# Half-height score matmuls for two heads into two PSUM banks side by side, in an attention kernel followed by two linear layers

One NeuronCore of one Trainium2 chip runs the whole program. The metric is the device time of one execution in microseconds (us); lower is better. The profile's span leaves out about 2 us of it. In the profile PE is TensorE (matmuls), ACT is ScalarE, DVE is VectorE and POOL is GpSimd. Matmuls write their results to a memory called PSUM, of which the pools below take eight banks; a pool hands out tiles, that is, named pieces of memory.

## The reference, cut to what matters

```python
def _attn_ref(q, k, v):                      # 8 batches, 8 heads, 576 positions, 64 per head
    scores = scale * np.matmul(q, k.transpose(0, 1, 3, 2))
    # heads 0 to 3: a band of 32 positions; heads 4 to 7: every 32nd position, causal
    scores = np.where(masks[None], scores, -1e9)
    ...                                      # softmax along the last axis
    return np.matmul(attn, v)

def _moe_ref(x, w_in, w_out, alpha):         # x: 4608 x 512, hidden 2048
    h = x @ w_in
    g = np.maximum(h, 0.0) + alpha * np.minimum(h, 0.0)
    return g @ w_out
```

The attention output, 4608 rows of 512, is the input of the two layers.

## The kernel before

Attention works on pairs of heads: a batch has two "local" pairs (6 blocks of 96 queries) and two "strided" ones (8 blocks of 72). Queries lie in `qpad`, where each head has its 64 rows and zeros in the other 64, so one matmul over 128 rows gives the scores of both heads:

```python
pspool = ...tile_pool(name="ps", bufs=5, space=PSUM)   # one bank each: tp, tt, sp, pv, xp
phpool = ...tile_pool(name="ph", bufs=2, space=PSUM)   # one bank each: first layer
popool = ...tile_pool(name="po", bufs=1, space=PSUM)   # second layer
# score_piece: 2 or 3 blocks, up to 432 columns, one bank
sp = pspool.tile([128, 512], F32, tag="ps", name="sp")
for x, t in enumerate(grp):
    matmul(sp[:, 2*w*x : 2*w*x + 2*w], P.kT[:, k0 : k0+128], P.qpad[:, :, w*t : w*t + w], ...)
...
activation(et[0:r, 0:n], sp[0:r, 0:n], AF.Exp, scale=SCALE)
# lin1_piece: 4 matmuls of 512 columns, then ReLU on ScalarE, then a fused op on VectorE
hps = phpool.tile([128, 512], F32, tag="hps", name="hps")
...
activation(neg, hps, AF.Relu, scale=-1.0)
scalar_tensor_tensor(gTs[n][:, m, :], neg, oma[:, m:m+1], hps, op0=mult, op1=add)   # a step later
```

In the dense part of the program a piece of the second layer, a step of attention, a piece of the first layer and another step of attention follow each other. A step of attention transposes q or k, makes scores, transposes an output, or multiplies weights by v (PV). Waits between engines are put in by the framework, from the tiles that each instruction reads and writes.

The softmax here doesn't subtract the row's maximum and nothing guards it: scores larger than these inputs give would overflow.

## Time and profile before

| | before |
|---|---|
| time | 373.56 us, median of 3 (372.94 to 374.19) |
| TensorE busy | 337.2 of 371.5 us (91%) |
| VectorE, ScalarE, POOL busy | 61%, 53%, 38% |
| chunk 0, chunk 1 of the first layer start | 36.99, 72.65 us |

A linear piece is one sixteenth of a chunk of 512 rows. The first is a line of the waits view: who waited for whom, us in total, times, longest. The second is TensorE's timeline (start, us, engine, line, what) near the end, where no attention is left.

```profile
PE hps L493 <- DVE gT L506: 0.7, 4, 0.2
```

```profile
295.41 1.03 PE L538 MATMUL ops<-wout,gT 128*128 128x512 f16 x4
296.27 1.03 PE L493 MATMUL hps<-xT,win 128*128 128x512 f16 x4
297.14 1.03 PE L538 MATMUL ops<-wout,gT 128*128 128x512 f16 x4
```

The first layer's two accumulators are enough: TensorE hardly ever waits for VectorE to empty one. One piece of each layer takes 297.14 - 295.41 = 1.73 us, with nothing between.

### The profile page before, as it was taken

The page shows a single profiled execution, that of the slowest core. Times are in us where ns is not written, and L with a number is a line of the kernel's source. Part 1 is how long each engine was busy: PE and PEld are TensorE (multiplying, and loading weights), DVE is VectorE, ACT ScalarE, POOL GpSimd, SP SyncE. Part 2 cuts the span into 40 slices and gives each one's busy share as a digit, 9 for nine tenths or more (in the row PEclk, how much of TensorE's full clock was granted, in tenths as well). Part 3 has the DMA queues.
Part 4 walks back from the last instruction along what each step waited for, and adds up shares of the span by engine and source line. Part 5 has one row for each costly group of instructions (what it writes and reads, how often), then busy time and mean ns, then how long its engine had stood idle before and what let it go on. Part 6 is the DMA issues. An engine that isn't in the chain of part 4 may idle for free.

```text
span 371.5 us, 6466 instructions
## 1 busy us (share of the span) xinstructions
PE 337.2 (91%) x2505; PEld 187.8 (51%) x2505; DVE 226.2 (61%) x442; ACT 195.4 (53%) x364; POOL 142.4 (38%) x189
## 2 busy tenths in 40 slices
PE   7677984897694999999999999999999999999996
PEld 2354443544452555555557767555555444444444
DVE  4265787488566567767776768685866544444410
ACT  2425675467345357564756585658565443353421
POOL 7274435204989364654655443335233000000000
PEclk9979998899999699999999999999999999999999
DMA  8999999915497377337535503100000001001012
GB/s 164 75 163 201 172 197 159 100 9 64 76 123 119 48 90 100 63 75 78 94 60 95 64 28 80 38 30 31 28 30 28 30 28 58 29 34 53 28 56 86
DMA packets 46779, 28.66 MB, mean 77 GB/s; under 512 B 27276, under 2 KB 41980, under 8 KB 46748
## 3 DMA queue, kind: packets, MB, share of 16 engines
q0 software_dynamic: 40944, 18.06, 43.6%
q1 hardware_dynamic: 5804, 10.19, 7.7%
q8 instruction: 19, 0.31, 0.4%
q14 instruction: 12, 0.10, 0.1%
HBM read 36.86 MB, written 9.44 MB: 125 GB/s over the span
## 4 chain that ended last, share of the span: by engine, by line
PE 72%; DMA 10%; ACT 6%; DVE 5%; POOL 4%; issue 2%; POOLq 0%; ACTq 0%
PE ops L538 30%; PE hps L493 29%; PE sp L287 4%; DMA k<-in_k_dram 3%; DMA wout<-in_moe_w_out_dram 3%; ACT kT L142 3%; PE pv L329 3%; PE tp L195 3%; DMA vl<-in_v_dram 2%; PE xp L346 2%; DMA q<-in_q_dram 2%; DVE x L338 2%; ACT neg L503 1%; PE ops L529 1%; DVE vl L144 1%
## 5 line engine op out<-in xcount | busy, mean ns | idle before, releaser
L493 PE MATMUL hps<-xT,win 128*128 128x512 f16 (+1 forms) x640 | 144.8, 359 | 1.0 <-DVE gT L506 0.7
L538 PE MATMUL ops<-wout,gT 128*128 128x512 f16 x560 | 142.9, 381 | 0.4 <-ACT osb L543 0.4
L506 DVE SCALAR_TENSOR_TENSOR gT<-neg,oma,hps 128x512 f16<-128x512 f32 x144 | 107.0, 743 | 53.5 <-ACT neg L503 50.0
L503 ACT ACTIVATE neg<-hps 128x512 f32<-128x512 f32 x144 | 86.0, 597 | 89.5 <-PE hps L493 87.7
L315 POOL TENSOR_TENSOR et<-et,consts 128x384 f16<-128x384 f16 (+2 forms) x60 | 54.3, 913 | 82.5 <-ACT et L307 81.7
L493 PEld LDWEIGHTS <-win 128*128 128x128 f16 x640 | 59.7, 98 | 50.0 <-issue 2.6
L538 PEld LDWEIGHTS <-gT 128*128 128x128 f16 x560 | 50.3, 98 | 46.1 <-issue 1.0
L307 ACT ACTIVATE et<-sp 128x384 f16<-128x384 f32 (+2 forms) x96 | 45.2, 489 | 23.7 <-PE sp L287 17.5
L287 PE MATMUL sp<-qpad,kT 128*128 128x144 f16 (+1 forms) x224 | 32.4, 241 | 13.9 <-DVE kT L144 4.5
L338 DVE TENSOR_TENSOR x<-pv,rc 72x384 f16<-72x384 f32 (+2 forms) x80 | 42.2, 527 | 2.7
L144 DVE COPY qpad<-tp 64x512 f16<-64x512 f16 (+1 forms) x44 | 37.7, 857 | 3.9 <-PE tp L195 1.9
L336 DVE RECIPROCAL rc<-pv 72x6 f32<-72x6 f32 (+2 forms) x80 | 14.8, 186 | 39.7 <-PE pv L329 39.5
L287 PEld LDWEIGHTS <-kT 128*128 128x128 f16 x224 | 20.0, 100 | 34.7 <-issue 7.3
L142 ACT COPY kT<-tp 64x512 f16<-64x512 f16 (+2 forms) x36 | 27.5, 765 | 14.8 <-PE tp L195 12.4
L329 PEld LDWEIGHTS <-et 72*128 72x128 f16 (+1 forms) x448 | 24.5, 100 | 20.9 <-issue 5.7
L543 ACT COPY osb<-ops 128x512 f32<-128x512 f32 x35 | 20.5, 586 | 20.1 <-PE ops L538 20.1
L560 PE MATMUL wps<-wrm 128*128 128x512 f16 x48 | 19.7, 479 | 1.2 <-DVE wrm L573 1.2
L102 POOL DMA_DIRECT2D q<-in_q_dram x16 | 11.9, 745 | 20.3 <-PE tp L195 15.1
L329 PE MATMUL pv<-vl,et 128*128 128x65 f16 x192 | 12.1, 195 | 6.3 <-DVE vl L144 3.8
L346 PE MATMUL xp<-consts,x 72*128 72x72 f16 (+1 forms) x224 | 15.5, 209 | 1.8 <-DVE x L338 1.7
L346 PEld LDWEIGHTS <-x 72*128 72x128 f16 (+1 forms) x224 | 12.9, 104 | 8.2 <-DVE x L338 3.1
L329 PE MATMUL pv<-vs,et 72*128 72x65 f16 x256 | 16.1, 199 | 0.1
(61 smaller groups left out, 205.9 us busy)
## 6 DMA issues: line engine op xcount, KB each, us to landing
out_dram<-osb SPq DMA_DIRECT2D x35, 256.0 KB, 2.0
q<-in_q_dram POOLq DMA_DIRECT2D x16, 256.0 KB, 5.3
k<-in_k_dram POOLq DMA_DIRECT2D x16, 256.0 KB, 5.9
vl<-in_v_dram POOLq DMA_DIRECT2D x8, 288.0 KB, 6.2
win<-in_moe_w_in_dram POOLq DMA_DIRECT2D x4, 512.0 KB, 8.2
wout<-in_moe_w_out_dram POOLq DMA_DIRECT2D x4, 512.0 KB, 13.0
stv<-in_v_dram POOLq DMA_DIRECT2D x7, 288.0 KB, 5.4
stv<-in_v_dram SPq DMA_DIRECT2D x1, 576.0 KB
```

The source lines that it names most:

```text
L142: keep(nc.scalar.copy(o, i))
L144: keep(nc.vector.tensor_copy(o, i))
L287: keep(nc.tensor.matmul(sp[:, 2 * w * x : 2 * w * x + 2 * w], P.kT[:, k0 : k0 + 128], P.qpad[:, :, w * t : w * t + w], start=(x == 0), sto ...
L307: keep(nc.scalar.activation(et[0:r, 0:n], sp[0:r, 0:n], AF.Exp, scale=SCALE))
L315: keep(nc.gpsimd.tensor_tensor(ev, ev, m.unsqueeze(1).to_broadcast([r, n // w, w]), op=ALU.mult))
L329: keep(nc.tensor.matmul(pv[:, 65 * x : 65 * x + 65], et[0:r, c : c + 128], v16[0:r, 2 * P.pr + hh, t, :] if P.strided else v16[:, 6 * (2 * ...
L338: keep(nc.vector.tensor_tensor(P.x16[0:w, c0 : c0 + 64 * nb].rearrange("r (c e) -> r c e", e=64), pvv[:, :, 0:64], rc[0:w, 0:nb].unsqueeze ...
L346: keep(nc.tensor.transpose(xp[:, P.w * t : P.w * t + P.w], P.x16[0 : P.w, 128 * t : 128 * t + 128], ident[0 : P.w, 0 : P.w]))
L493: keep(nc.tensor.matmul(hps[:, dst : dst + w], win16[:, kk, 128 * m : 128 * m + 128], xT[:, kk, src : src + w], start=(kk == 0 and x == 0) ...
L503: keep(nc.scalar.activation(neg, hps, AF.Relu, scale=-1.0))
L506: keep(nc.vector.scalar_tensor_tensor(gTs[n][:, m, :], neg, oma[:, m : m + 1], hps, op0=ALU.mult, op1=ALU.add))
L538: keep(nc.tensor.matmul(ops, gTs[n][:, kf, 128 * mt : 128 * mt + 128], wout16[:, kf, :], start=(kf == 0), stop=(kf == 15)))
```

## The change

It wants fewer and larger instructions around the scores. Heads of a pair sit in rows 0 to 63 and 64 to 127 of a compact `qT`, and each gets its own matmul of half height into its own bank; one exponential and one mask multiplication then cover both banks, 576 columns of each pair at a time, twice per pair instead of three times. Copies into a padded q go. Local q and k come in as fp32 and are cast on POOL; memsets, loads and the order of attention pieces change too. Because a score block takes two banks, the eight banks are dealt out anew.

```diff
-    pspool = ... tile_pool(name="ps", bufs=5, PSUM)
-    phpool = ... tile_pool(name="ph", bufs=2, PSUM)
+    pspool = ... tile_pool(name="ps", bufs=3, PSUM)
+    phpool = ... tile_pool(name="ph", bufs=1, PSUM)
+    pbpool = ... tile_pool(name="pb", bufs=1, PSUM)
+    sb = pbpool.tile([128, 2, 512], F32, name="sb")
+    hb = phpool.tile([128, 2, 512], F32, name="hb")
 ... (score_piece)
-        sp = pspool.tile([128, 512], F32, tag="ps", name="sp")
+        sp = hb if wide["on"] and ectr["i"] % 2 else sb
-            matmul(sp[:, 2*w*x : 2*w*x + 2*w], P.kT[:, k0 : k0+128], P.qpad[:, :, w*t : w*t+w], ...)
+            for y in range(2):
+                hf = slice(64*y, 64*y + 64)
+                matmul(sp[:, y, w*x : w*x + w], P.kT[hf, k0 : k0+128], P.qT[hf, w*t : w*t+w], ...)
-        activation(et[0:r, 0:n], sp[0:r, 0:n], AF.Exp, scale=SCALE)
+        activation(ev.rearrange("r (y c) -> r y c", y=2), sp[0:r, :, 0:n], AF.Exp, scale=SCALE)
 ... (lin1_piece)
-            hps = phpool.tile([128, 512], F32, tag="hps", name="hps")
+            hps = hb[:, m % 3 if alone else m % 2]
 ... (copies, loads, casts, memsets, order of pieces: cut)
```

`wide` is on while attention runs with no linear layer beside it.

More of the change, by code (lines that the diff above doesn't have):

```diff
@@ L27, in _build_consts @@
     ident = np.eye(128, dtype=np.float16)
-    return np.concatenate([ident, first, first, other, other, mstr], axis=1)
+    return np.concatenate([ident, first, other, other, mstr], axis=1)
 @with_exitstack
@@ L62 @@
     opool = ctx.enter_context(tc.tile_pool(name="op", bufs=3))
-    pspool = ctx.enter_context(tc.tile_pool(name="ps", bufs=5, space=bass.MemoryType.PSUM))
-    phpool = ctx.enter_context(tc.tile_pool(name="ph", bufs=2, space=bass.MemoryType.PSUM))
+    pspool = ctx.enter_context(tc.tile_pool(name="ps", bufs=3, space=bass.MemoryType.PSUM))
+    phpool = ctx.enter_context(tc.tile_pool(name="ph", bufs=1, space=bass.MemoryType.PSUM))
+    pbpool = ctx.enter_context(tc.tile_pool(name="pb", bufs=1, space=bass.MemoryType.PSUM))
     popool = ctx.enter_context(tc.tile_pool(name="po", bufs=1, space=bass.MemoryType.PSUM))
@@ L72 @@
     ))
-    consts = cpool.tile([128, 584], F16)
+    consts = cpool.tile([128, 488], F16)
     id16 = cpool.tile([16, 16], F32)
@@ L76 @@
     oma = cpool.tile([128, 16], F32)
-    madd = cpool.tile([128, 456], F16)
+    madd = cpool.tile([128, 360], F16)
     ident = consts[:, 0:128]
-    mfirst, mother, mstr = consts[:, 128:512], consts[:, 320:416], consts[0:72, 512:584]
+    mfirst, mother, mstr = consts[:, 128:416], consts[:, 224:320], consts[0:72, 416:488]
     win16 = cpool.tile([128, 4, 2048], F16)
@@ L83 @@
     xT = cpool.tile([128, 4, RING], F16)
-    NE = 8
-    qpads = [cpool.tile([128, 2, 2, S], F16, name=f"qpad{i}") for i in range(2)]
+    NE = 6
+    qTs = [cpool.tile([128, 2, S], F16, name=f"qT{i}") for i in range(2)]
     kTs = [cpool.tile([128, 2, 672], F16, name=f"kT{i}") for i in range(2)]
@@ L89, with load_qk, cast_l @@
     vss = [cpool.tile([128, 4, 8, 65], F16, name=f"vs{i}") for i in range(2)]
-    ets = [cpool.tile([128, 512], F16, name=f"et{i}") for i in range(NE)]
+    ets = [cpool.tile([128, 640], F16, name=f"et{i}") for i in range(NE)]
     loaded = {}
     cast16 = {}
-    def load_qk(b, strided):
+    def load_qk(b, strided, nm):
         h0 = 4 if strided else 0
-        for nm, src in (("q", q), ("k", k)):
-            t16 = hpool.tile([128, 2, 512], F16, tag=f"{nm}16", name=f"{nm}16")
-            base = src[b, h0 : h0 + 1, 0:1, :]
-            keep(nc.gpsimd.dma_start(t16, bass.AP(
-                tensor=base.tensor, offset=base.offset,
-                ap=[[8 * D, 64], [2 * S * D, 2], [S * D, 2], [1, 8 * D]])))
-            cast16[(b, strided, nm)] = t16
+        src = q if nm == "q" else k
+        if strided:
+            t16 = hpool.tile([128, 2, 512], F16, tag=f"{nm}s", bufs=3, name=f"{nm}s")
+            cast16[(b, True, nm)] = t16
+        else:
+            t16 = hpool.tile([128, 2, 512], F32, tag=f"{nm}l", bufs=2, name=f"{nm}l")
+            loaded[(b, nm)] = t16
+        base = src[b, h0 : h0 + 1, 0:1, :]
+        eng = nc.sync if b > 2 and not strided else nc.gpsimd
+        keep(eng.dma_start(t16, bass.AP(
+            tensor=base.tensor, offset=base.offset,
+            ap=[[8 * D, 64], [2 * S * D, 2], [S * D, 2], [1, 8 * D]])))
+    def cast_l(b, nm, eng="pool"):
+        t16 = hpool.tile([128, 8, 2, 64], F16, tag=f"{nm}l16", bufs=2, name=f"{nm}l16")
+        cast_copy(eng, t16, loaded[(b, nm)].rearrange("p f (t d) -> p t f d", t=8))
+        cast16[(b, False, nm)] = t16
     def load_tail(b, strided):
@@ L165 @@
     ectr = {"i": 0}
-    q_rest = []
+    wide = {"on": True}
+    sb = pbpool.tile([128, 2, 512], F32, name="sb")
+    hb = phpool.tile([128, 2, 512], F32, name="hb")
     NEARLY = 2
@@ L175, in make_pair @@
         u = g // 2
-        P.qpad, P.kT = qpads[u % 2][:, g % 2], kTs[u % 2][:, g % 2]
-        P.sgroups = ([0, 1, 2], [3, 4, 5], [6, 7]) if P.strided else ([0, 1], [2, 3], [4, 5])
-        P.pgroups = P.sgroups if P.strided else ([0, 1, 2], [3, 4, 5])
+        P.qT, P.kT = qTs[u % 2][:, g % 2], kTs[u % 2][:, g % 2]
+        P.sgroups = ([0, 1, 2, 3], [4, 5, 6, 7]) if P.strided else ([0, 1, 2], [3, 4, 5])
+        P.pgroups = ([0, 1, 2], [3, 4, 5], [6, 7]) if P.strided else P.sgroups
         P.et = {}
@@ L190, in transpose_piece @@
         src = cast16[(b, strided, nm)]
-        qpad, kT = qpads[u % 2], kTs[u % 2][:, :, 32:608]
+        dst = qTs[u % 2] if nm == "q" else kTs[u % 2][:, :, 32:608]
         tp = pspool.tile([128, 8, 64, 2], F16, tag="ps", name="tp")
         for j in range(8):
-            t, f = j // 2, j % 2
-            keep(nc.tensor.transpose(
-                tp[:, j].rearrange("r p e -> r (p e)"), src[:, f, 128 * t : 128 * t + 128], ident))
-        half = [slice(0, 64), slice(64, 128)]
+            blk = (src[:, j % 2, 128 * (j // 2) : 128 * (j // 2) + 128] if strided
+                   else src[:, j].rearrange("p f d -> p (f d)"))
+            keep(nc.tensor.transpose(tp[:, j].rearrange("r p e -> r (p e)"), blk, ident))
@@ L199, in transpose_piece @@
         if strided:
             main = tp.rearrange("r j p e -> r e j p")
-            def q_copy(par, es, eng):
-                o = qpad[half[par], es, par, :].rearrange("r e (j p) -> r e j p", j=8)
-                cast_copy(eng, o[:, :, :, 0:64], main[half[par], es])
-            def k_copy(es, eng):
-                o = kT[:, es].rearrange("r e (j p) -> r e j p", j=8)
-                cast_copy(eng, o[:, :, :, 0:64], main[:, es])
-        else:
-            main = tp.rearrange("r (t f) p e -> r f e p t", f=2)
-            def q_copy(f, par, eng):
-                o = qpad[half[f], :, f, 0:512].rearrange("r e (p t c) -> r e p t c", t=4, c=2)
-                cast_copy(eng, o[:, :, :, :, par], main[half[par], f])
-            def k_copy(f, par, eng):
-                o = kT[half[f], :, 0:512].rearrange("r e (p t c) -> r e p t c", t=4, c=2)
-                cast_copy(eng, o[:, :, :, :, par], main[half[par], f])
@@ L222, in transpose_piece @@
-        e0, e1, both = slice(0, 1), slice(1, 2), slice(0, 2)
-        if nm == "q":
-            if strided and early:
-                q_copy(0, e0, "dve")
-                q_copy(1, e0, "act")
-                q_rest.append(lambda: (q_copy(0, e1, "dve"), q_copy(1, e1, "act")))
-            elif strided:
-                q_copy(0, both, "dve")
-                q_copy(1, both, "dve")
-            else:
-                for f in range(2):
-                    for par in range(2):
-                        q_copy(f, par, "act" if early and par else "dve")
+            o = dst.rearrange("r e (j p) -> r e j p", j=8)[:, :, :, 0:64]
+        else:
+            main = tp.rearrange("r t p e -> r e p t")
+            o = dst[:, :, 0:512].rearrange("r e (p t) -> r e p t", t=8)
@@ L235, in transpose_piece, with tails @@
+        if early:
+            for e in range(2):
+                eng = "dve" if (nm == "q") == (e == 0) else "act"
+                if nm == "k" and e == 1:
+                    tails(b, u, strided)
+                cast_copy(eng, o[:, e : e + 1], main[:, e : e + 1])
             return
+        cast_copy("dve" if nm == "q" else "act", o, main)
+        if nm == "k":
+            tails(b, u, strided)
+    def tails(b, u, strided):
         tl = cast16[(b, strided, "tail")]
@@ L246, in transpose_piece @@
                     tt[:, 128 * e : 128 * e + 128], tl[:, 128 * e : 128 * e + 128], ident))
-        def tails():
+        for i, (o, eng) in enumerate(((qTs[u % 2], "dve"), (kTs[u % 2][:, :, 32:608], "act"))):
             if strided:
                 tv = tt[:, 0:256].rearrange("r (e f i p t) -> r i e t f p", e=2, f=2, i=2, p=8)
-                ov = lambda o: o.rearrange("r e (t f p) -> r e t f p", t=4, f=2)
+                ov = o.rearrange("r e (t f p) -> r e t f p", t=4, f=2)
                 for e in range(2):
-                    keep(nc.scalar.copy(ov(kT)[:, e, :, :, 64:72], tv[:, 1, e]))
-                for par in range(2):
-                    for e in range(2):
-                        keep(nc.vector.tensor_copy(
-                            ov(qpad[half[par], :, par, :])[:, e, :, :, 64:72],
-                            tv[half[par], 0, e]))
+                    cast_copy(eng, ov[:, e, :, :, 64:72], tv[:, i, e])
@@ L259, in tails @@
             else:
                 tv = tt[:, 0:256].rearrange("r (e i p) -> r i e p", e=2, i=2)
-                keep(nc.scalar.copy(kT[:, :, 512:576], tv[:, 1]))
-                for f in range(2):
-                    keep(nc.vector.tensor_copy(qpad[half[f], :, f, 512:576], tv[half[f], 0]))
-        if strided and early:
-            k_copy(e0, "act")
-            tails()
-            q_rest.pop()()
-            k_copy(e1, "dve")
-        elif strided:
-            k_copy(both, "act")
-            tails()
-        else:
-            for f in range(2):
-                for par in range(2):
-                    k_copy(f, par, "dve" if early and par else "act")
-            tails()
+                cast_copy(eng, o[:, :, 512:576], tv[:, i])
@@ L279, in score_piece @@
     def score_piece(P, i):
         et = ets[ectr["i"] % NE]
+        sp = hb if wide["on"] and ectr["i"] % 2 else sb
         ectr["i"] += 1
-        sp = pspool.tile([128, 512], F32, tag="ps", name="sp")
-        w = P.w
-        grp = P.sgroups[i]
+        w, grp = P.w, P.sgroups[i]
+        n = w * len(grp)
+        r = 72 if P.strided else 128
+        early = P.b < NEARLY
         for x, t in enumerate(grp):
             k0 = 32 + 72 * t if P.strided else 96 * t
-            keep(nc.tensor.matmul(
-                sp[:, 2 * w * x : 2 * w * x + 2 * w], P.kT[:, k0 : k0 + 128],
-                P.qpad[:, :, w * t : w * t + w], start=(x == 0), stop=(x == len(grp) - 1 and P.b >= NEARLY),
-                skip_group_check=True))
@@ L291, in score_piece @@
             for y in range(2):
+                hf = slice(64 * y, 64 * y + 64)
+                keep(nc.tensor.matmul(
+                    sp[:, y, w * x : w * x + w], P.kT[hf, k0 : k0 + 128],
+                    P.qT[hf, w * t : w * t + w], start=(x == 0),
+                    stop=(x == len(grp) - 1 and not early), skip_group_check=True))
                 key = (2 * (t // 2) + y, t % 2) if P.strided else (t, y)
-                P.et[key] = (et, 2 * w * x + w * y)
-        n = 2 * w * len(grp)
@@ L296, in score_piece @@
-        r = 72 if P.strided else 128
+                P.et[key] = (et, n * y + w * x)
         first = not P.strided and i == 0
-        if P.b < NEARLY:
+        if early:
             if first:
-                m = madd[:, 0:384]
+                m = madd[:, 0:288]
             else:
-                m = madd[0:72, 384:456] if P.strided else madd[:, 192:288]
+                m = madd[0:72, 288:360] if P.strided else madd[:, 96:192]
                 m = m.unsqueeze(1).to_broadcast([r, n // w, w])
-            keep(nc.tensor.matmul(
-                sp[:, 0:n], ident[0:r, :], m, start=False, stop=True, skip_group_check=True))
@@ L307, in score_piece @@
-        keep(nc.scalar.activation(et[0:r, 0:n], sp[0:r, 0:n], AF.Exp, scale=SCALE))
-        if P.b < NEARLY:
+            for y in range(2):
+                keep(nc.tensor.matmul(
+                    sp[:, y, 0:n], ident[0:r, :], m, start=False, stop=True, skip_group_check=True))
+        ev = et[0:r, 0 : 2 * n]
+        keep(nc.scalar.activation(
+            ev.rearrange("r (y c) -> r y c", y=2), sp[0:r, :, 0:n], AF.Exp, scale=SCALE))
+        if early:
             return
         if first:
-            keep(nc.gpsimd.tensor_tensor(et[:, 0:n], et[:, 0:n], mfirst, op=ALU.mult))
-        else:
-            m = mstr if P.strided else mother
-            ev = et[0:r, 0:n].rearrange("r (c f) -> r c f", f=w)
-            keep(nc.gpsimd.tensor_tensor(
-                ev, ev, m.unsqueeze(1).to_broadcast([r, n // w, w]), op=ALU.mult))
+            ev = ev.rearrange("r (y c) -> r y c", y=2)
+            m = mfirst.unsqueeze(1).to_broadcast([r, 2, n])
+        else:
+            ev = ev.rearrange("r (c f) -> r c f", f=w)
+            m = (mstr if P.strided else mother).unsqueeze(1).to_broadcast([r, 2 * n // w, w])
@@ L318, in pv_piece @@
+        keep(nc.gpsimd.tensor_tensor(ev, ev, m, op=ALU.mult))
     def pv_piece(P, a):
@@ L380, in alone @@
         for g in A:
-            for i in range(3):
+            for i in range(2):
                 feed(Sc(g, i), -1)
+        feed(T(u1, "q"), -1)
         for i in range(3):
             feed(Pv(A[0], i), -1)
-        feed(T(u1, "q"), -1)
+        feed(T(u1, "k"), -1)
         for i in range(3):
             feed(Pv(A[1], i), -1)
-        feed(T(u1, "k"), -1)
-        feed(X(A[0]), -1)
-        for i in range(3):
-            feed(Sc(L[0], i), -1)
-        feed(X(A[1]), -1)
-        for i in range(3):
-            feed(Sc(L[1], i), -1)
+        for g in L:
+            for i in range(2):
+                feed(Sc(g, i), -1)
+            feed(X(A[g - L[0]]), -1)
         for g in L:
@@ L431 @@
             seq.append(("Tk", T(t // 2, "k"), t))
-        if okA:
-            seq.append(("S", Sc(a, 2), a))
         if nP == 3:
@@ L437 @@
         todo = [(g // 4, pr) for pr in range(2)] if g % 4 == 0 and 8 <= g < npair else []
+        if g % 4 == 1 and 9 <= g and g // 4 + 1 < B:
+            todo = [(g // 4 + 1, nm) for nm in "qk"]
         lastP = max([i for i, s in enumerate(seq) if s[0][0] == "P"], default=-1)
@@ L451, in run @@
                 for b, pr in extra:
+                    if pr in ("q", "k"):
+                        cast_l(b, pr)
+                        if b + 1 < B:
+                            load_qk(b + 1, False, pr)
+                        continue
                     cast_v(b, pr, "pool")
@@ L455, in run @@
                 if kind == "Tk" and u // 2 + 2 < B:
-                    load_qk(u // 2 + 2, u % 2 == 1)
+                    if u % 2 == 1:
+                        load_qk(u // 2 + 2, True, "q")
+                        load_qk(u // 2 + 2, True, "k")
                     load_tail(u // 2 + 2, u % 2 == 1)
@@ L516, in lin2_piece @@
             if last and mt % 2 == 1:
-                ops_cur["t"] = phpool.tile([128, 512], F32, tag="hps", name="ops2")
+                ops_cur["t"] = hb[:, 0]
             else:
@@ L526, in lin2_piece @@
             c0 = 128 * part
-            half = phpool.tile([128, 512], F32, tag="hps", name="ops3") if part else ops
+            half = hb[:, 1] if part else ops
             for kf in range(16):
@@ L564, with load_unit @@
     wps = popool.tile([128, 512], F32, tag="ops", name="wps")
-    load_qk(0, True)
+    def load_unit(b, strided, v_too=True):
+        load_qk(b, strided, "q")
+        load_qk(b, strided, "k")
+        load_tail(b, strided)
+        if v_too:
+            load_v(b, strided)
+    keep(nc.vector.memset(wrm, 0.0))
+    load_qk(0, True, "q")
     keep(nc.sync.dma_start(consts, consts_dram))
-    load_tail(0, True)
     load_v(0, True)
     keep(nc.sync.dma_start(alpha_r, moe_alpha.rearrange("(kf p) -> kf p", p=128)))
-    load_qk(0, False)
-    load_tail(0, False)
-    load_v(0, False)
-    keep(nc.vector.memset(wrm, 0.0))
+    load_qk(0, True, "k")
+    load_tail(0, True)
     for i in range(2):
-        keep(nc.vector.memset(qpads[i][64:128, :, 0, :], 0.0))
-        keep(nc.vector.memset(qpads[i][0:64, :, 1, :], 0.0))
         keep(nc.vector.memset(kTs[i][:, :, 0:32], 0.0))
         keep(nc.vector.memset(kTs[i][:, :, 608:672], 0.0))
-    keep(nc.gpsimd.memset(vss[0][:, :, :, 64:65], 1.0))
+    for t in ets:
+        keep(nc.vector.memset(t[:, 576:640], 0.0))
     keep(nc.gpsimd.memset(vls[0][0:32, 0:1, 0:64], 0.0))
     keep(nc.gpsimd.memset(vls[0][:, :, 64:65], 1.0))
-    for t in ets:
-        keep(nc.gpsimd.memset(t[:, 288:512], 0.0))
+    keep(nc.gpsimd.memset(vss[0][:, :, :, 64:65], 1.0))
+    load_unit(0, False)
+    for c in range(2):
+        load_w(c, False)
     keep(nc.gpsimd.memset(vls[1][0:32, 0:1, 0:64], 0.0))
@@ L586 @@
     keep(nc.gpsimd.memset(vss[1][:, :, :, 64:65], 1.0))
-    for c in range(4):
-        load_w(c, False)
-    load_qk(1, True)
-    load_tail(1, True)
-    load_v(1, True)
-    load_qk(1, False)
-    load_tail(1, False)
-    load_v(1, False)
-    for c in range(4):
-        load_w(c, True)
+    cast_l(0, "q")
+    load_w(2, False)
+    cast_l(0, "k")
+    load_unit(1, True, False)
+    load_w(3, False)
+    load_v(1, True)
+    load_unit(1, False)
     warm(12)
+    keep(nc.vector.tensor_copy(id16, ident[0:16, 0:16]))
     keep(nc.vector.tensor_scalar(
-        madd, consts[:, 128:584], -1.0, 30000.0, op0=ALU.add, op1=ALU.mult))
+        madd, consts[:, 128:488], -1.0, 30000.0, op0=ALU.add, op1=ALU.mult))
     cast_v(0, 0, "act")
@@ L605 @@
     for i in range(end0):
-        if i == 12:
-            keep(nc.vector.tensor_copy(id16, ident[0:16, 0:16]))
+        if i == 1:
             keep(nc.tensor.transpose(apt[:, 0:16], alpha_r, id16))
@@ L621, in attn_n @@
             attn_step(0)
-    load_qk(2, False)
-    load_tail(2, False)
-    load_v(2, False)
-    load_qk(2, True)
-    load_tail(2, True)
+    wide["on"] = False
+    for c in range(4):
+        load_w(c, True)
+    cast_l(1, "q")
+    cast_l(1, "k")
+    load_unit(2, False)
+    load_unit(2, True, False)
     for m in range(16):
         lin1_piece(0, m, True)
-        attn_n(0 if m < 13 else 1, end1)
+        attn_n(0 if m < 9 else 1, end1)
         if m == 12:
             cast_v(1, 0, "act")
-        if m == 14:
-            cast_v(1, 1, "dve")
+        if m == 13:
+            cast_v(1, 1, "act")
             load_v(2, True)
+    wide["on"] = True
     while pos["i"] < end1:
         attn_step(end1)
-    for strided in (False, True):
-        load_qk(3, strided)
-        load_tail(3, strided)
-    load_v(3, False)
+    wide["on"] = False
+    cast_l(2, "q")
+    cast_l(2, "k")
+    load_unit(3, False)
+    load_unit(3, True, False)
     end2 = attn_until(2)
@@ L645 @@
         lin1_piece(1, m, True)
-        attn_n(0 if m < 14 else 1, end2)
+        attn_n(0 if m < 13 else 1, end2)
     for i in range(16):
         lin2_piece(0, i)
-        attn_n(2, end2)
+        attn_n(2 if i % 2 else 1, end2)
+    for i in range(8):
+        lin2_piece(1, i)
+        attn_n(1, end2)
     while pos["i"] < end2:
         attn_step(end2)
-    for n in range(1, NCH):
+    end3 = attn_until(3)
+    for m in range(16):
+        lin1_piece(2, m)
+        attn_n(1, end3)
+        if m % 2:
+            lin2_piece(1, 8 + m // 2)
+            attn_n(2, end3)
+    while pos["i"] < end3:
+        attn_step(end3)
+    for n in range(2, NCH):
         ab = attn_until(n + 2) if n + 2 < B else len(pieces)
```

## The prediction

> **What bounds the kernel now.** I read the slices of the page first, then the waits of every engine, then TensorE's timeline from start to end.
>
> ```profile
> PE   7677984897694999999999999999999999999996
> PEclk9979998899999699999999999999999999999999
> DMA  8999999915497377337535503100000001001012
> ```
>
> A slice is 371.5 / 40 = 9.3 us. From slice 14 (about 130 us) TensorE is full to the end; before that it is not, although it also runs 48 warm-up matmuls that compute nothing. So there are two regimes. After 130 us only TensorE's own work counts. Before it, waits count, and the waits view names them:
>
> ```profile
> ACT qpad L142 <- DVE qpad L144: 10.4, 7, 2.8
> POOL vl L581 <- DMA vl<-in_v_dram: 6.7, 1, 6.7
> PE sp L287 <- DVE kT L144: 4.5, 2, 2.7
> ACT et L307 <- POOL et L583: 4.0, 1, 4.0
> PE sp L287 <- ACT kT L142: 3.6, 2, 2.1
> ```
>
> Columns: who waited for whom, us in total, times, longest. The first scores wait for exponentials, those for the memsets of `et` on POOL, and POOL sits behind a memset of `vl` that waits for a load. Local scores wait for the copies of q and k, which VectorE and ScalarE make in turns out of one bank. The timeline of TensorE (start, us, what) gives the milestones and the price of a piece:
>
> ```profile
> 29.59 0.34 PE L287 MATMUL sp<-qpad,kT 128*128 128x192 f16 x2 [1.73 <-DVE kT L144]
> 36.99 8.20 PE L493 MATMUL hps<-xT,win 128*128 128x512 f16 x36
> 72.65 13.38 PE L493 MATMUL hps<-xT,win 128*128 128x512 f16 x60
> ...
> 87.18 0.61 PE L195 MATMUL tp<-consts,k 128*128 128x128 f16 x8
> 87.63 0.28 PE L245 MATMUL tt<-consts,tl 128*128 128x128 f16 x2
> ...
> 122.77 1.90 PE L538 MATMUL ops<-wout,gT 128*128 128x512 f16 x4
> ...
> 160.87 0.33 PE L287 MATMUL sp<-qpad,kT 128*128 128x192 f16 x2
> 161.04 1.03 PE L493 MATMUL hps<-xT,win 128*128 128x512 f16 x4
> 161.90 0.35 PE L329 MATMUL pv<-vl,et 128*128 128x65 f16 x6
> 162.08 1.03 PE L538 MATMUL ops<-wout,gT 128*128 128x512 f16 x4
> 162.95 0.61 PE L195 MATMUL tp<-consts,k 128*128 128x128 f16 x8
> 163.49 0.29 PE L240 MATMUL tt<-consts,tl 64*128 64x64 f16 x4
> 163.71 1.04 PE L493 MATMUL hps<-xT,win 128*128 128x512 f16 x4
> ...
> 165.61 0.35 PE L287 MATMUL sp<-qpad,kT 128*128 128x144 f16 x3
> 165.80 1.03 PE L493 MATMUL hps<-xT,win 128*128 128x512 f16 x4
> ```
>
> Durations overlap; the price is the distance between starts. A linear piece (4 matmuls of 512 columns) costs 161.90 - 161.04 = 0.86 us, so 16 of them 13.8 us. A local score piece costs 0.17 us, a strided one 0.19, and six PV matmuls of 65 columns with six weight loads 0.18, or 0.03 each: that is what one small matmul with its own load costs. Milestones: the first layer's chunk 0 starts at 36.99, chunk 1 at 72.65, and the dense stage with two layers interleaved at about 122.8. The rest of it is arithmetic: 8 chunks of layer two and 7 of layer one (15 x 13.8 = 207 us) plus attention of five batches plus 3.5 us after the last matmul end at 371.5, so a batch of attention costs TensorE (371.5 - 122.8 - 207 - 3.5) / 5 = 7.6 us.
>
> **What the Trainium skill says.** "TensorEngine Tiling (Array Packing)", Key Properties: "Mode switching requires drain", while tiles operate independently. The trace before has one such switch, the 64-row transposes `tt` of strided units. From `tp` to `tt` takes 0.54 us at 162.95, against 0.45 at 87.18 where `tt` has 128 rows; and its four matmuls take 0.22 us where 4 x 0.03 = 0.12 would do. So going in and out costs 0.09 + 0.10 = 0.19 us: the page is confirmed, and this is its price. "TensorE: Matmul & The Clock Gate", The mechanism (Part 3): a weight load overlaps matmuls in flight in another row group, so two half-height matmuls can run together. No run here shows it yet. "PSUM — Partial Sum Buffer", PSUM bank collisions: ScalarE and VectorE may not read one bank together; the 10.4 us of ACT waiting for DVE on `qpad` agree.
>
> **The change part by part.**
>
> *Scores on TensorE.* Per pair 8 or 6 blocks become 16 or 12 half-height matmuls of 72 or 96 columns, in two pieces instead of three. The column time halves at best, but each matmul has its own weight load, and the loads are serial at 0.03 us. A strided piece: 8 x 0.03 + 0.19 (in and out) = 0.43 us, two of them 0.86, against 0.19 + 0.19 + 0.13 = 0.50 for the three before: +0.36. A local piece: 6 x 0.03 to 0.04 (96 columns alone are 0.04) + 0.19 = 0.37 to 0.43, two 0.74 to 0.86, against 3 x 0.17 = 0.51: about +0.3. A batch has two pairs of each: +1.3, say +1.4 us with the second gap inside the mode. In the stage where TensorE is full this lies wholly on the path. Batches 2 to 7: 6 x 1.4 = +8.4 us.
>
> *Exponentials and masks.* ScalarE's rows are 405 ns at 288, 492 at 384 and 526 at 432 columns: 0.84 ns a column and 163 fixed, so 576 columns take about 650 ns. 64 x 650 = 41.6 us against 45.2: -4 us of an engine that is not the bound. POOL: 731 ns at 288, 1000 at 432, so about 1.27 us at 576; two per pair, 2.5 instead of 2.7. POOL gains 16 casts of local q and k, which I take as 1.1 us each from its copy of 72x1024 in 1.04. Nothing of this is on TensorE's path when TensorE is full.
>
> *Copies.* Without padding, q is one copy of 1024 elements (VectorE's row: 1219 ns for 64x1024) in place of two, or of four of 722 ns; likewise k on ScalarE. In the first two batches it is two copies of 512 columns, 0.6 to 0.7 us each, still one after the other because of the bank: 1.4 us in place of 3 us for q and again for k. These are on the path of batches 0 and 1.
>
> *Start.* The `et` memsets go to VectorE and the `vl` memsets ahead of their load. The exponentials ran from 16.57 us; the first scores were there at 11.4, so that wait of some 5 us goes. q local lands at 10.6 us and k at 12.8 (before), plus a cast each: ready at about 12 and 14. Step by step from there: strided scores 11 to 14.3 (four exponentials of 0.65 with masks and semaphores), q local transposed 14.3, three PV pieces, k local 16.5, its copies done 18.5 to 19; four local score pieces 3.6 us, four PV pieces at VectorE's 0.74 (190 + 550 ns) 3 us, output transposes: chunk 0 of layer one starts at about 26 instead of 37. Loads allow it: the queue no longer pauses from 16.1 to 18.3, so the first weights land at 18.7, 21.2 and 23.8.
>
> *Batch 1.* Seven attention pieces lie inside chunk 0 (three before): 13.8 + 4.4 + 1.5 of hitches, to 45.7. The 19 others: six PV pieces and k's copies 5 us, scores 3, PV 2 to 3 more: about 10.5 us, where the part from the first PV took 16.4 before. Chunk 1 starts at 56.5 instead of 72.65: 16 us gained.
>
> *Batch 2.* It is spread over 24 second-layer pieces instead of 16: 24 x 0.86 + 7.6 + 1.4 + about 4.5 of stalls (before: 35 - 13.8 - 7.6 = 13.7) = 34. From 56.5: chunk 1 with its attention 15, then 34: 105.5.
>
> *Dense stage and end.* 7.5 chunks of layer two and 7 of layer one 200 us, five batches x 9.0 = 45, end 3.5, extra stalls from fewer banks 1: 249.5. Sum 355 us of span. The reported time was 373.56 for a span of 371.5, so add 2: 357 us.
>
> **Rivals.** (a) Concurrency pays more than I allow, or the switch is hidden behind a 512-column matmul: then scores cost nothing extra and the time is 349. Against it: `tp` to `tt` shows the drain bare, and PV shows loads at 0.03 us. (b) The start gains little because loads set it: queues are 90% busy up to 70 us, and chunk 0 needs its fourth weight block, now queued behind half of batch 1 (about 30 us). Then chunk 1 starts near 65 and the time is 366. Against it: before, the weights had landed by 31.5 and TensorE waited for copies afterwards. (c) One `sb` buffer of two banks and three instead of five `ps` banks put a wait in every score piece. For it: an exponential and its semaphores hold `sb` for about 1 us. Against: in the dense stage the next score piece is at least two slots of 1.05 us away. At 0.2 us in 48 pieces it would be +10: 367. (d) POOL with its casts becomes the bound of batch 2, as its 8 to 9 tenths in slices 10 to 12 suggest: +4.
>
> **Range and chances.** The two big terms, -16 at the start and +8.4 for the switches, are each uncertain by about 40%; the stalls of batch 2 by 4 us. Together about +-9: 347 to 367. Faster by over 2% means below 366.1: 0.88; within 2%: 0.09; slower: 0.03.
>
> **What would show it.** In the profile after: a gap of about 0.1 us at each side of a score piece in the dense stage, score matmuls 0.03 us apart, a batch's score share near 3.4 us instead of 2.0; exponentials near 650 ns; chunk 0 from about 26 us and chunk 1 from 56; no wait on `et` memsets. I am wrong if chunk 1 starts after 65, if the dense stage shows waits for `et` before scores, or if a period of the dense stage (35.4 us, 148.37 to 183.77) does not grow.

## The result

The changed kernel took 441.45 us, median of 4 (440.39 to 442.23), against 373.88 for the kernel before. The ratio is 1.1796, with a 95% interval of 1.1737 to 1.1856; here and below a ratio is the mean time of one kernel's fast runs over that of the other's in the same rounds, so not quite the ratio of the medians. Executions over 1.5% slower than the fastest of the same kernel are left out of the means. The results were correct. The prediction had said 357 us, faster with a chance of 0.88; the kernel is 18% slower.

The slices of its page, 440.5 / 40 = 11.0 us each:

```profile
PE   7986785679996766999899989988987777777795
PEclk9989979899999998999999999999999999999999
DMA  8999998002964560554345200000000100000011
```

The clock is granted almost throughout and loads are over early. Yet TensorE, which before stood at 9 from slice 14 on, stays at 7 where no attention is left at all (slices 31 to 38, counted from 1, that is from 330 us; the last score matmul starts at 317.0). There at least the cause lies in the two layers, not in the scores. The waits view of the same run:

```profile
ACT neg L486 <- PE hb L476: 170.6, 124, 4.2
DVE gT L489 <- ACT neg L486: 138.1, 92, 3.1
PE hb L476 <- DVE gT L489: 65.7, 100, 2.0
```

The last line answers to the 0.7 us of before: TensorE waits 100 times for VectorE's `gT` before it may start a first-layer piece. Together the three lines are a ring: TensorE to ScalarE to VectorE to TensorE. All engines' timeline shows one turn of it, with no attention piece inside it:

```profile
295.17 1.02 PE L476 MATMUL hb<-xT,win 128*128 128x512 f16 x4 [0.34 <-DVE gT L489]
...
296.03 1.03 PE L521 MATMUL ops<-wout,gT 128*128 128x512 f16 x4
296.23 0.60 ACT L486 ACTIVATE neg<-hb 128x512 f32<-128x512 f32 x1 [1.37 <-PE hb L476]
...
296.86 0.75 DVE L489 SCALAR_TENSOR_TENSOR gT<-neg,oma,hb 128x512 f16<-128x512 f32 x1 [1.74 <-ACT neg L486]
...
297.66 1.02 PE L476 MATMUL hb<-xT,win 128*128 128x512 f16 x4 [0.60 <-DVE gT L489]
```

The piece at 297.66 writes the other half of `hb` than the one at 295.17. Still it starts only when the fused operation of the piece before it ends (296.86 + 0.75 = 297.61). A turn takes 2.49 us instead of 1.73. The bracket shows 0.60 us of waiting where 0.76 are lost: a matmul's modelled duration (379 ns) covers 0.16 us after the next one could have started (216 ns), so this wait is counted short by that. If every wait is, 100 waits cost about 65.7 + 100 x 0.16 = 82 us; that is an estimate.

### The profile page after: what moved, and what is told of

The parts are those of the page before. It is cut to its first block, busy times and chain, and to the rows that moved or that the text cites. A ratio compares the mean times of both kernels' runs of the same rounds, so it can differ in the third digit from the quotient of the medians.

```text
span 440.5 us, 6757 instructions
## 1 busy us (share of the span) xinstructions
PE 356.5 (81%) x2733; PEld 179.9 (41%) x2733; DVE 197.3 (45%) x389; ACT 178.4 (41%) x309; POOL 144.9 (33%) x163
## 4 chain that ended last, share of the span: by engine, by line
PE 48%; DVE 29%; ACT 14%; issue 4%; POOL 3%; DMA 1%; ACTq 0%; POOLq 0%
PE hb L476 30%; DVE gT L489 20%; ACT neg L486 11%; PE ops L521 7%; DVE x L315 5%; PE pv L306 2%; PE tp L211 2%; DVE rc L313 2%; DMA qs<-in_q_dram 1%; ACT kT L154 1%; POOL et L293 1%; PE wps L543 1%; PE xp L323 1%; DVE qT L156 1%; DVE xT L331 1%
## 5 line engine op out<-in xcount | busy, mean ns | idle before, releaser
L476 PE MATMUL hb<-xT,win 128*128 128x512 f16 (+1 forms) x600 | 140.1, 360 | 67.8 <-DVE gT L489 65.7
L489 DVE SCALAR_TENSOR_TENSOR gT<-neg,oma,hb 128x512 f16<-128x512 f32 x134 | 99.6, 744 | 134.1 <-ACT neg L486 134.0
L486 ACT ACTIVATE neg<-hb 128x512 f32<-128x512 f32 x134 | 80.0, 597 | 173.2 <-PE hb L476 170.6
L293 POOL TENSOR_TENSOR et<-et,consts 128x576 f16<-128x576 f16 (+1 forms) x48 | 61.1, 1274 | 113.0 <-ACT et L283 112.9
L283 ACT ACTIVATE et<-sb 72x576 f16<-72x576 f32 (+1 forms) x58 | 37.5, 647 | 22.0 <-PE sb L264 14.7
L264 PEld LDWEIGHTS <-kT 64*128 64x128 f16 x448 | 11.0, 96 | 25.3 <-issue 18.2
L156 DVE COPY qT<-tp 128x1024 f16<-128x1024 f16 (+1 forms) x16 | 17.4, 1085 | 8.8 <-PE tp L211 8.8
L264 PE MATMUL sb<-qT,kT 64*128 64x72 f16 (+1 forms) x408 | 17.8, 203 | 1.1 <-ACT kT L154 1.0
L154 ACT COPY kT<-tp 128x1024 f16<-128x1024 f16 (+1 forms) x16 | 14.5, 906 | 9.3 <-PE tp L211 9.3
L146 POOL DMA_DIRECT2D vl<-in_v_dram x8 | 9.7, 1210 | 10.5 <-DVE rc L313 6.3
```

The costliest lines, as they stand in the source:

```text
L156: keep(nc.vector.tensor_copy(o, i))
L264: keep(nc.tensor.matmul(sp[:, y, w * x : w * x + w], P.kT[hf, k0 : k0 + 128], P.qT[hf, w * t : w * t + w], start=(x == 0), stop=(x == len( ...
L283: keep(nc.scalar.activation(ev.rearrange("r (y c) -> r y c", y=2), sp[0:r, :, 0:n], AF.Exp, scale=SCALE))
L293: keep(nc.gpsimd.tensor_tensor(ev, ev, m, op=ALU.mult))
L476: keep(nc.tensor.matmul(hps[:, dst : dst + w], win16[:, kk, 128 * m : 128 * m + 128], xT[:, kk, src : src + w], start=(kk == 0 and x == 0) ...
L486: keep(nc.scalar.activation(neg, hps, AF.Relu, scale=-1.0))
```

## The experiments

The diffs are cut to the lines that matter; where a run makes the same exchange for the second layer's tiles of the last chunk, that is left out.

**Theory A:** the waits treat the two halves of `hb` as one buffer, so the double buffering of the first layer is gone. **Theory B:** the score blocks cost it: switches of TensorE's mode, two-bank exponentials, three `ps` buffers instead of five.

### e1_split: separate accumulators

```diff
-    phpool bufs=1;  hb = phpool.tile([128, 2, 512], F32)
+    phpool bufs=2
-        sp = hb if wide["on"] and ectr["i"] % 2 else sb
+        sp = sb
-            hps = hb[:, m % 3 if alone else m % 2]
+            hps = phpool.tile([128, 512], F32, tag="hps", name="hps")
```

> The changed kernel with one part undone: the first layer's accumulators are again two separate one-bank tiles, and score blocks use the two-bank tile sb alone. Theory A (the two halves of hb are waited for as one buffer, so each first-layer piece waits for ReLU and the fused multiply-add of the piece before it): the wait of the first layer on VectorE's gT falls from 65.7 us in 100 waits to under 5 us, two linear pieces without attention take 1.73 us again instead of 2.49, and the time is 345 to 360 us. Theory B (score blocks cost it: mode switches, exponentials over two banks, three ps buffers instead of five): still above 420 us.

Measured: 361.17 us, ratio 0.9631 (0.9582 to 0.968). No line of a first-layer piece waiting for `gT` is left in TensorE's waits. The largest is the price of scoring into one block only:

```profile
PE sb L263 <- ACT et L282: 4.8, 9, 0.7
```

Two linear pieces without attention take 307.94 - 306.21 = 1.73 us again. The time is 1 us above the range that I had given theory A; theory B is refuted as the cause of the loss, since all that it names is still in this kernel.

### e2_before_onetile: the same fault put into the kernel before

```diff
+    hb = phpool.tile([128, 2, 512], F32, name="hb")      # phpool: bufs=1
-            hps = phpool.tile([128, 512], F32, tag="hps", name="hps")
+            hps = hb[:, m % 3 if alone else m % 2]
```

> The kernel before, with one edit: its two one-bank accumulators of the first layer become the two halves of one two-bank tile, used in turn as before. Nothing of the scores changes. Theory A: the same wait appears, and the time rises from 374 to 425 to 445 us. Theory B: 374 us within 1%.

Measured: 477.0 us (472.94 to 479.47), ratio 1.2716. The direction is A's, the size was underestimated by 32 us or more.

```profile
PE hb L494 <- DVE gT L507: 77.4, 117, 2.2
```

There are more such waits than in the changed kernel, 117 against 100. Counted with the 0.16 us that the view leaves out they give about 77.4 + 117 x 0.16 = 96 us, and the spans differ by 471.1 - 371.5 = 99.6. This kernel has no half-height score matmul and no block of 576 columns, so neither is needed for the loss.

### f1_flat: is it the form of the slice?

```diff
-    hb = phpool.tile([128, 2, 512], F32, name="hb")
+    hbt = phpool.tile([128, 1024], F32, name="hb");  hb = hbt.rearrange("p (y c) -> p y c", y=2)
-            hps = hb[:, m % 3 if alone else m % 2]
+            hps = hbt[:, 512 * (...) : 512 * (...) + 512]        # (...) as in the line above
```

> The changed kernel with hb declared flat, 128 by 1024, and its halves taken as column ranges 0 to 512 and 512 to 1024; nothing else. If the program's waits go by the columns that a slice names, and only the three-dimensional form of hb hid them, the time falls to about 356 us. If a PSUM tile is waited for as one whole however it is cut, it stays at 441 us.

Measured once, state unknown: 438.56 us, beside 375.37 for the kernel before. What settles it is not the single time but the wait, which is there as in the change (65.7 us in 100):

```profile
PE hb L477 <- DVE gT L490: 66.3, 101, 2.0
```

How the half is written makes no difference.

### e3_scoped and e3_again: the change, repaired

The two banks change hands in time: a two-bank tile while attention runs alone, then its pool is closed and one with two one-bank tiles opened, and so on.

```diff
+    def enter_phase(wide_on):                 # closes the pool before, opens the next
+        phase["pool"] = tile_pool(bufs=1 if wide_on else 2, space=PSUM)
+        phase["hb"] = phase["pool"].tile([128, 2, 512], F32) if wide_on else None
-        sp = hb if wide["on"] and ectr["i"] % 2 else sb
+        sp = phase["hb"] if wide["on"] and ectr["i"] % 2 else sb
-            hps = hb[:, m % 3 if alone else m % 2]
+            hps = phase["pool"].tile([128, 512], F32, tag="hps", name="hps")
```

> The changed kernel with the two banks of hb handed over in time: one two-bank tile while attention runs alone (scores alternate between it and sb as in the change), two one-bank tiles while the first layer runs. Theory A: as e1_split, and up to 3 us faster, because the early score blocks need not wait for the exponential before them: 343 to 358 us. Theory B: above 420 us.

> The repaired change (e3_scoped) once more, with more rounds, because its four runs spread from 352.0 to 358.5 us: 353 to 357 us, a ratio of 0.94 to 0.95.

Measured: 355.35 us (351.95 to 358.5; the run of 358.5 counts as slow and is not in the ratio), ratio 0.945 (0.939 to 0.9511); again, six fast runs, 355.7 us (353.47 to 356.88), ratio 0.9487 (0.9446 to 0.9529). It beats both kernels: 5% faster than before. Its timeline without attention is that of before again, 1.72 us for two pieces:

```profile
295.31 1.03 PE L487 MATMUL hps<-xT,win 128*128 128x512 f16 x4
296.17 1.03 PE L532 MATMUL ops<-wout,gT 128*128 128x512 f16 x4
297.03 1.03 PE L487 MATMUL hps<-xT,win 128*128 128x512 f16 x4
```

It is 361.17 - 355.7 = 5.5 us faster than e1_split, more than the 3 that I allowed; the wait of scores for exponentials falls from 4.8 to 0.4 us. The span of the changed kernel is 440.5 - 354.0 = 86.5 us longer than this one's, against the 82 counted from the waits; the other 4 us I have not traced.

### e4_full_height and x5_full_late: what do half-height matmuls cost?

e4 is e1_split with padded q and all 128 rows in each matmul:

```diff
-                matmul(sp[:, y, ...], P.kT[hf, k0 : k0+128], P.qT[hf, w*t : w*t+w], ...)
+                matmul(sp[:, y, ...], P.kT[:, k0 : k0+128], P.qT[:, y, w*t : w*t+w], ...)
+        # and q copied into the padded tile in two halves of 64 rows,
+        # whose zeros four memsets on VectorE write at the start
```

> e1_split with q padded again, so that the same score matmuls (two heads into two banks, blocks of 576 columns) run over all 128 rows and TensorE never changes its mode for scores. Trace of the change: a visit of a score piece takes 0.095 us to enter and 0.235 to the next piece, 0.33 in all; at full height I expect 8 x 0.03 = 0.24 or 6 x 0.04 = 0.24. Eight pieces a batch: 0.7 us less a batch, 4 us less over batches 2 to 7, against 2 us more at the start for q's copies in halves. If switches cost what the trace says: 1 to 4 us faster than e1_split. If running two heads at once is worth more than the switch: slower than e1_split by 2 us or more.

Measured: 368.2 us, ratio 0.9815 (0.9779 to 0.9852), so 7 us slower than e1_split instead of faster. The windows view tells matmuls and copies apart. It gives a stretch, its length, then busy time and instructions of each engine, clock, DMA share and GB/s. First one batch of the dense stage at full height, then one of e3_scoped:

```profile
191.16:226.42 35.26, 35.12 (x374) 25.61 (x372) 25.33 (x50) 20.13 (x35) 18.56 (x18) 1.00 0.40 65
```

```profile
177.96:213.56 35.60, 35.58 (x374) 24.25 (x371) 22.50 (x45) 20.06 (x35) 18.55 (x18) 1.00 0.41 64
```

Where TensorE is full, full height is even 0.34 us a batch cheaper, half of the 0.7 expected. The 7 us are lost earlier: chunk 1 of the first layer starts at 69.11 us instead of 64.43, the second layer at 87.9 instead of 82.1 and chunk 2 at 121.46 instead of 115.29. Among TensorE's waits are some for copies that e1_split has smaller (1.3 us for the first line) or not at all (the second):

```profile
PE pv L309 <- ACT qT L154: 2.2, 1, 2.2
...
PE hps L479 <- DVE qT L156: 1.2, 1, 1.2
```

x5 combines the two: e3_scoped with padded, full-height scores in batches 2 to 7 alone.

```diff
-                matmul(sp[:, y, ...], P.kT[hf, ...], P.qT[hf, ...], ...)
+                matmul(sp[:, y, ...], P.kT[hf, ...] if early else P.kT[:, ...],
+                       P.qT[hf, ...] if early else P.qP[:, y, ...], ...)
+        # q of batches 2 to 7 copied in two halves, and four memsets of qP on POOL
```

> e3_scoped with full-height score matmuls on padded q in batches 2 to 7 only, and half-height ones with compact q in batches 0 and 1. In the stage where TensorE is full a batch took 35.2 us at full height (e4_full_height) and 35.5 at half height (e3_scoped); six batches give 2 us, and the start, where e4_full_height lost 6 us to copies of q in halves, stays as in e3_scoped. So 2 us faster than e3_again, 353 us. If the loss of e4_full_height came from the matmuls and not from the copies, it is slower than e3_again.

Measured: 356.41 us, ratio 0.9503 (0.947 to 0.9536), the same as e3_again within the intervals; the 2 us did not come. A dense batch did take 35.11 us, against 177.64 - 142.18 = 35.46 in e3_again. But from the last first-layer piece of chunk 1 to the first of chunk 3 (starts in the timelines) it took 144.42 - 75.20 = 69.2 us, against 142.18 - 74.80 = 67.4 in e3_again: the denser stage before lost 1.8 us, and from there to the end of the span x5 gained only 1.3 (210.2 us against 211.5). Most of that loss can be read from the timelines, first e3_again, then x5:

```profile
135.63 1.23 DVE L167 COPY qT<-tp 128x1024 f16<-128x1024 f16 x1 [0.53 <-PE tp L222]
136.77 1.40 DVE L500 SCALAR_TENSOR_TENSOR gT<-neg,oma,hps 128x512 f16<-128x512 f32 x2
137.57 1.89 PE L487 MATMUL hps<-xT,win 128*128 128x512 f16 x8
```

```profile
136.59 2.46 DVE L168 COPY qP<-tp 64x1024 f16<-64x1024 f16 x2 [0.53 <-PE tp L224]
139.08 1.40 DVE L514 SCALAR_TENSOR_TENSOR gT<-neg,oma,hps 128x512 f16<-128x512 f32 x2
139.88 1.89 PE L501 MATMUL hps<-xT,win 128*128 128x512 f16 x8 [1.34 <-DVE gT L514]
```

A copy of 64 rows takes as long as one of 128, so q in halves holds VectorE for 2.46 us instead of 1.23; the fused operations start 2.49 us after the copies do instead of 1.14, and TensorE waits 1.34 us where it did not wait before. For this wait the copies are the cause. The rest of the 1.8 us, and the part of the copies in e4's loss at the start, are argued and not isolated.

### x1_before_memsets: does the start reach the end?

```diff
-    for t in ets: gpsimd.memset(t[:, 288:512], 0.0)          # behind vl's load
+    for t in ets: vector.memset(t[:, 288:512], 0.0)
     # and the two memsets of vls[0] moved ahead of load_v(0, False)
```

> The kernel before with one piece of the change's start alone: the memsets of et go to VectorE, and those of vl stand ahead of its load. If what is gained at the start reaches the end, the first exponential starts at about 11.7 us instead of 16.57 and the time falls by 4 to 5 us, to about 369.5. If loads or the copies of q and k take the gain back, it stays within 1.5 us of 374.

Measured: 371.12 us against 375.16, ratio 0.9916 (0.9878 to 0.9954): under 2%, but clear of 1. The first exponential starts at 12.40 us, and chunk 0 of the first layer at 32.24 instead of 36.99. Of these 4.75 us about 4.0 reach the end (1.7 to 4.6 by the interval), the low end of the forecast: the start lies on the path, and loads do not take the gain back.

## Why the prediction was wrong, and where it was right

| us of the span | predicted | changed kernel | repaired (e3_scoped) |
|---|---|---|---|
| chunk 0 of layer one starts | 26 | 26.8 | 26.7 |
| chunk 1 starts | 56.5 | 69.3 | 58.5 |
| batch 2 done, chunk 2 starts | 105.5 | 130.9 | 109.6 |
| from there to the end | 249.5 | 309.6 | 244.4 |
| span | 355 | 440.5 | 354.0 |

**The step that failed** is the term "extra stalls from fewer banks 1" of the dense stage, and the same silent term in batches 1 and 2. The working priced each linear piece at 0.86 us and took it for granted that `hb[:, m % 2]` is still two buffers because it is two banks. It is one tile, and the waits went by the tile. e1_split and e2_before_onetile settle this: take the shared tile out and the loss goes, put it alone into the old kernel and it comes. The loss is some 82 us where the term said 1. One of the prediction's own signs of being wrong came, chunk 1 after 65 us (69.3), but not because of loads, as rival (b) had it: with the same loads e3_scoped starts it at 58.5. Rival (c) looked for a wait of this kind, but at `sb` and worth 10 us. None of the four rivals priced the ring of first layer, ReLU and fused operation, although its numbers were in the profile of before: 0.86 + 0.60 + 0.75 us and the gaps between engines make 2.49 us a turn.

The sums of the prediction, redone, hold to 0.3 us.

**The start** was right: chunk 0 within 1 us in both kernels, and x1_before_memsets shows one part of it reaching the end. *Batch 1* was right in kind; in the repaired kernel chunk 1 started 2 us later than the sum.

**The switch of mode** was priced right, and the matmuls between were priced too dear. In e3_scoped a score piece stands between two linear pieces like this:

```profile
186.41 1.02 PE L532 MATMUL ops<-wout,gT 128*128 128x512 f16 x4
187.37 0.30 PE L275 MATMUL sb<-qT,kT 64*128 64x72 f16 x8
187.61 1.05 PE L487 MATMUL hps<-xT,win 128*128 128x256 f16 x8
```

Entering costs 187.37 - 186.41 - 0.86 = 0.10 us, as forecast. But the eight matmuls and the way out together take 187.61 - 187.37 = 0.24 us, not 8 x 0.03 + 0.10 = 0.34. In the trace's single records, which this view merges, the two matmuls of a block start 3 to 4 ns apart, their weight loads 3 ns, and the next pair follows 0.03 to 0.04 us later. So pairs run together, as "TensorE: Matmul & The Clock Gate", The mechanism (Part 3), has it for different row groups. Four pairs take some 0.14 us, which leaves the forecast 0.10 for the way out. The step that failed here is "the loads are serial": it is the concurrency of rival (a), though the switch itself was not hidden. A visit is 0.33 us instead of 0.43, a batch's scores 8 x 0.33 = 2.64 instead of 3.4, or +0.64 over the 2.0 of before instead of +1.4. And the dense batch grew by only 0.1 us, from 35.40 and 35.48 to 35.60 and 35.47, since the start-to-start distances of the PV pieces, with the small waits behind them, fell from 2.26 to 1.73 us a batch. So of the +8.4 us almost nothing came.

**Exponentials and masks** came out as worked out: 647 ns (forecast 650) and 1274 ns (1.27 us); the casts took 1051 and 1035 ns (1.1 us). VectorE's copy of 1024 elements took 1217 ns.

**The range** was worked out from the terms that were in the sum. That the repaired kernel, 355.7 us, lands within 2 us of the 357 forecast is partly luck: a dearer batch 2 (51.1 us from chunk 1 to chunk 2, forecast 49) was made up by the cheaper switches.

What stays open: why the framework's waits take a two-bank PSUM tile as one, and whether it does so in every case. It does not do so with every tile: in the kernel before, ScalarE and VectorE write two parts of one tile `vs`, which is not in PSUM, at the same time (casts from 6.79 and 6.80 us, of 1.05 and 0.69). And in the runs with separate tiles these were also drawn anew from the pool for each piece, while `hb` lives on; no run kept two lasting one-bank tiles. That the chip doesn't need the wait when the two accumulators lie in two banks is shown: separate tiles gave correct results without it.

## What to carry to other kernels

Double buffering is a matter of what the waits distinguish, not of how many banks there are: when buffers are merged into one tile, look whether writer and reader of different halves still overlap, and price the whole ring (fill, read, read again) in case they don't. A line of the waits view that is near zero before, such as 0.7 us for `gT`, names a protection that a change can remove. When a forecast rests on a resource being re-dealt, put the loss of each buffer among the rivals, with its own number.

## What the Trainium skill lacked or had wrong

- "PSUM — Partial Sum Buffer", Summary: rules for kernel authors, says to guard PSUM by bank. It does not warn that a program whose waits go by tile turns two banks of one tile into one buffer: 65.7 us of waits in 100 cases here, and 77.4 in 117 when only the tiles of the old kernel were merged.
- "TensorEngine Tiling (Array Packing)", Key Properties, says that a mode switch drains, without a price. Here entering costs 0.10 us, leaving about as much (estimate above), and a visit of eight half-height matmuls of 72 columns 0.33 us in all.
- "Perfetto Trace Analysis", Tensor Engine Instruction, says that a matmul's end is estimated. What follows from it is missing: idle time before a matmul is counted short, by 0.16 us a wait here (0.60 shown, 0.76 lost).
